# The first token half of a Winograd feed-forward: weight preparation placed at other steps, one subtraction on another engine, and an interleaved last period

## The chip, the cores and the metric

One core of a Trainium2 chip runs the whole block. The metric is the device time of one execution in microseconds. TensorE (PE) multiplies, VectorE (DVE), ScalarE (ACT) and GpSimd (POOL) do the element work, and SyncE (SP) issues almost all DMAs from one queue, in order.

## The reference

```python
mod = (_silu(c) @ w_mod).reshape(c.shape[0], 6, 1, -1)
sa, ca, ga, sb, cb, gb = (mod[:, j] for j in range(6))
h = _layernorm(x, axis=-1) * (1 + ca) + sa
x = x + ga * _A_ref(h, A_wq, A_wk, A_wv, A_wo, A_beta)     # segmented attention with a memory
h = _layernorm(x, axis=-1) * (1 + cb) + sb
x = x + gb * ((_silu(h @ B_w_gate) * (h @ B_w_up)) @ B_w_down)
```

There are 2048 tokens of width 576, and the feed-forward is 4608 wide. All data are float32. The attention fills about the first 650 us. The change lies in the feed-forward, which fills the rest, and in the last few microseconds ahead of it.

## The kernel before

**Two token halves, 18 periods each.** The feed-forward runs over token halves t = 0 and 1 (1024 tokens each). A period p takes 256 of the 4608 columns. In it, z = 0 is the gate and z = 1 the up projection. Each is computed as a 2 x 2 block product by the Strassen-Winograd scheme: seven products m = 1 to 7 in place of eight, each of a sum of activation blocks with a sum of weight blocks. So a period has 14 steps, k = 0 to 13, seven for z = 0 and then seven for z = 1. In the first half the order is `MO0 = (1, 2, 6, 7, 4, 5, 3)`, in the second `MO7 = (1, 5, 6, 2, 7, 4, 3)`.

**A product.** `prod` issues seven matmuls of 512 columns. A float32 operand is split into a rounded part and a remainder (`wh` and `wl` for weights; the activations `y` hold both), which gives three matmuls for each of two 128-row blocks, and one more for the last 32 rows, whose parts are packed in `wr`. In the first half the result goes to one of four PSUM banks `M` in rotation, and DVE (`sg`, `tb`, `tc`, `cu`, lines 1150 to 1191) or ACT (`tb`, line 1180, at m = 1) reads it. Combining the products gives the four blocks of the gate (`sg`, with a SiLU on ACT) and of the up projection; the gate times the up projection (L1159) is the input of the down projection, split into `ah` (ACT, L1226) and `al` (DVE, L1227) by `prep_a`.

**The down projection of a period runs in the next one.** In the first half `plain` issues it as 8 chunks of 12 matmuls of 288 columns, one chunk in each of steps 4 to 11; after each, DVE adds the result to `acc` (L1287). So steps 4 to 11 are long for PE and steps 0 to 3, 12 and 13 short. In the second half `down` uses the Winograd scheme (14 chunks of 6 matmuls), but for the last two periods.

**Weight preparation in the first half.** For each z, `load_o` fetches four raw weight blocks into `O` (two buffers); `sum_o` (four operations on POOL, L1091) makes the three sums. `prep_w` casts one operand to `wh` (ACT, L1100) and leaves the subtraction `wl` (DVE, L1101) in a list `later`, which is run at the start of the next step; it works `PF = 5` steps ahead with `WR = 8` buffers. `prep_r` casts the last rows into `wr` (ACT, L1085), and the subtraction of its 32 remainder rows runs on POOL (L1086). For the down weights, `load_d` fetches, `mul_d` scales them (POOL, L1114), `sum_d` makes sums for the second half (POOL, L1119), and `prep_d` casts `dh` (ACT) and subtracts `dl` (DVE, L1126) into a ring of 8. `store_o`, `store_r` and a store of `RW` write the sums to DRAM (`oD`, `rD`, `wdD`), where the second half reads them, so POOL has no work there.

**The second half's activations.** Also during the first half, the generator `prep2` normalizes the second token half, transposes it on PE (into a bank `M`), splits it and stores it in DRAM (`yD`). It is advanced by one piece at steps `G2` of periods 1 to 17, and its rest is run at the start of period 17. In period 17, once the z = 1 product m has used its operand, `load_y` overwrites that part of `y` with the second half's.

**What sets the order.** The order of the instructions on every engine is the order in which the program issues them, written out by hand, step by step. A tile ring makes a new tile wait for the readers of the one that it replaces. SP's queue holds each DMA until its operands are ready, and everything behind it waits too.

The steps of the first half, as the main loop has them (the work that a later listing moves is shown alone):

```python
if k == 7 - PF:
    load_o(tn, nx, 0)
elif k == 14 - PF:
    load_o(tn, nx, 1)
if tn == 0 and 4 <= k < 8:
    sum_o(nx, 0, k - 4)
elif tn == 0 and k >= 11:
    sum_o(nx, 1, k - 11)
elif k == 0 and p:
    sum_o(p, 1, 3)
```

Of the kernel before, what the change touches and what calls it, by code (L numbers as in the profile page):

```python
# [11 lines left out]
ALU = mybir.AluOpType  # L12
# [20 lines left out]
MO = [0, 76, 228, 380, 532]  # L33
WR = 8
PF = 5
NSG = 7
CH = (1, 1, 1, 1, 2, 1, 0, 1, 1, 1, 1, 2, 1, 0)
# [32 lines left out]
def f32(ap):  # L70
    return ap.bitcast(F32)
# [3 lines left out]
def block(ctx: ExitStack, tc: tile.TileContext, x, wqk, wv, wo, beta, wgu, wd, c, w_mod, out):  # L75
# [8 lines left out]
    def chain(*g):  # L84
        for a in g:
            yield from a
# [992 lines left out]
    def prep_r(t, p, z):  # L1079
        R[z] = r = wrp.tile([P, 7, P], F32R, tag="wr", name="wr")  # L1080
        if t == 1:
            nc.sync.dma_start(f32(r[0:96]), rD[p][z])
            return
        o = O[p, z]
        nc.scalar.copy(r[0:96], o[0:96, :, 2, :])  # L1085
        later.append(lambda: nc.gpsimd.tensor_tensor(r[32:64], o[32:64, :, 2, :], f32(r[32:64]), op=ALU.subtract))  # L1086

# [79 lines left out]

    def fin0(z, ij, bank, add):
        fin(z, ij, bank, add)
        if z:  # L1170
            prep_a(par[0], ij, AC[ij])

    par = [0]

    def step0(z, m):
        bank = ps.tile([P, L], F32, tag="M", name=f"M{m}", bufs=4)
        prod(z, m, bank, True, True)
        if m == 1:
            T[0] = tmp("tb")
            nc.scalar.copy(T[0], bank)  # L1180
        elif m == 2:
            fin0(z, (0, 0), bank, T[0])
        elif m == 6:
            nc.vector.tensor_tensor(T[0], bank, T[0], op=ALU.add)
        elif m == 7:
            T[1] = tmp("tc")
            nc.vector.tensor_tensor(T[1], bank, T[0], op=ALU.add)
        elif m == 4:
            fin0(z, (1, 0), bank, T[1])
        elif m == 5:  # L1190
            nc.vector.tensor_tensor(T[0], bank, T[0], op=ALU.add)
            fin0(z, (1, 1), bank, T[1])
        else:
            fin0(z, (0, 1), bank, T[0])

# [77 lines left out]
    def plain(t, p, c):  # L1273
# [25 lines left out]
    with tc.manual_schedule():  # L1299
# [49 lines left out]
        load_o(0, 0, 1)  # L1349
        gt, gw = chain(tr[1], tr[2]), iter(MO0[:PF])  # L1350
        for i in range(4):
# [34 lines left out]
        x2p = pool(p6, "x2p")  # L1386
        ps = pool(p6, "psm", 1, space=PSUM)
# [4 lines left out]
        seq = [(t, p, z, m) for t in range(2) for p in range(NPR) for z in range(2) for m in (MO7 if t else MO0)]  # L1392
        prev = None
        n = 0
        for p in range(NPR):
            nx = (p + 1) % NPR
            tn = 0 if nx else 1
            par[0] = p % 2
            if p == NPR - 1:
                run(g2)  # L1400
            for k in range(14):
                z, m = k // 7, MO0[k % 7]
# [8 lines left out]
                if k == 7 - PF:  # L1411
                    load_o(tn, nx, 0)
                elif k == 14 - PF:
                    load_o(tn, nx, 1)
                if tn == 0 and 4 <= k < 8:
                    sum_o(nx, 0, k - 4)
                elif tn == 0 and k >= 11:
                    sum_o(nx, 1, k - 11)
                elif k == 0 and p:
                    sum_o(p, 1, 3)  # L1420
                if k == 0 and p == 0:
                    store_o(p, 0)
                elif k == 9 and tn == 0:
                    store_o(nx, 0)
                elif k == 3:
                    store_r(p, 0)
                    store_o(p, 1)
                elif k == 6:
                    store_r(p, 1)
                if k == 2:  # L1430
                    prep_r(0, p, 1)
                elif k == 9:
                    prep_r(tn, nx, 0)
                if prev is not None and DS <= k < DS + 8:
                    plain(*prev, k - DS)
                if k == 1:
                    load_d(0, p)
                elif k in (5, 6):
                    mul_d(p, k - 5)
                elif 8 <= k < 12 and p < NPR - 2:  # L1440
                    sum_d(p, k - 8)
                elif k == 13:
                    nc.sync.dma_start(wdD[p][:, :NS[p]], RW[p][:, :NS[p]])
                if 8 <= k < 12:
                    prep_d(p, ((k - 8) // 2, k % 2), k - 8)
# [8 lines left out]
        ps = pool(p4, "ps4", 1, space=PSUM)  # L1454
        for p in range(NPR):
            last = p == NPR - 1
# [4 lines left out]
            for k in range(14):  # L1461
                z, m = k // 7, MO7[k % 7]
                todo, later[:] = later[:], []
                if n + PF < len(seq):
                    prep_w(*seq[n + PF][1:])
                n += 1
# [33 lines left out]
                if is_plain(1, p):  # L1500
                    if k in (4, 5, 6, 7):
                        prep_d(p, ((k - 4) // 2, k % 2), k - 4)
                elif k >= 7:
                    prep_d(p, POS[k - 7], WSLOT[POS[k - 7]])
                for ij, kk, j in (((0, 0), 11, 1), ((1, 1), 12, 4), ((1, 0), 13, 2)):
                    if k == kk:
                        prep_a(p % 2, ij if is_plain(1, p) else j, AC[ij])
            PA.clear()
            PA.update(AC)
# [59 lines left out]
```

## Time and profile before

| what | us |
|---|---|
| runs: median (lowest to highest) | 1984.6 (1984.16 to 1990.09) |
| the profiled execution | 1984.65 |
| its span | 1982.9 |
| PE busy in the span | 1893.7 |
| DVE busy | 1596.6 |
| ACT busy | 889.1 |
| POOL busy | 649.0 |
| `wl` on DVE, L1101, 504 of them | 298.8 |
| `wr` subtraction on POOL, L1086, 36 of them | 77.1 |
| sums of `O` on POOL, L1091, 144 of them | 161.9 |

The span is the time from the first to the last instruction of the core; the rest of an execution's time lies around it. A busy time says how long an engine had an instruction in it, also one that was held up, so a long busy time is not all work. A matmul's time overlaps that of its neighbours. To see what limits a stage, read it by itself: the first half of the feed-forward runs from 656 to 1334 us of the span, the second from there to the end.

In the page's view of the span in 40 equal slices (49.6 us each), PE and DVE in tenths are:

```
PE   7999999999998799999999999988999999999998
DVE  7574267877886899998998989984888888888886
```

DVE is at 8 to 9 tenths in the first half's slices (14 to 26), and PE dips in slices 27 and 28, where the halves meet.

### The profile page before, as it was taken

The numbers are of one execution on the slowest core, as the hardware profiler recorded it, in microseconds if no ns is written. First come the engines' busy times: TensorE is split into PE (matmuls) and PEld (weight loads), VectorE is DVE, ScalarE is ACT, GpSimd is POOL, SyncE is SP. The second block draws the span as 40 slices with busy tenths as digits, with TensorE's granted clock in tenths as the row PEclk, the third lists the DMA queues.
The fourth block names the chain that finished last, engine by engine and source line by source line (L and its number), as shares of the span: only waits on it lengthen the run. The fifth ranks groups of instructions, "written<-read, shape, count | busy, mean of one in ns | idle before, by whom it ended". The sixth has DMA issues, their size and how long they took to land.

```text
span 1982.9 us, 31199 instructions
## 1 busy us (share of the span) xinstructions
PE 1893.7 (96%) x10927; PEld 1564.1 (79%) x10927; DVE 1596.6 (81%) x3375; ACT 889.1 (45%) x1928; POOL 649.0 (33%) x808
## 2 busy tenths in 40 slices
PE   7999999999998799999999999988999999999998
PEld 4888856676766688888888877877888888888888
DVE  7574267877886899998998989984888888888886
ACT  2222267767666343344344343333444544454442
POOL 5212235554536556556556645520000000000000
PEclk9999999999999899999999999998999999999999
DMA  7777564445435554464555545477434334343441
GB/s 226 245 232 248 204 177 130 140 137 156 129 100 146 203 186 163 158 207 144 195 159 164 195 140 163 149 234 255 148 126 145 127 128 143 105 148 112 147 148 48
DMA packets 147052, 322.63 MB, mean 163 GB/s; under 512 B 26256, under 2 KB 61456, under 8 KB 145424
## 3 DMA queue, kind: packets, MB, share of 16 engines
q1 hardware_dynamic: 144640, 314.71, 49.3%
q10 hardware_dynamic: 2256, 5.93, 0.8%
q8 instruction: 86, 1.41, 0.3%
q14 instruction: 70, 0.57, 0.1%
HBM read 201.80 MB, written 118.75 MB: 162 GB/s over the span
## 4 chain that ended last, share of the span: by engine, by line
PE 71%; DVE 17%; DMA 5%; issue 3%; ACT 3%; POOL 1%; SPq 0%; ACTq 0%; DVEq 0%; POOLq 0%
PE A L1136 12%; PE pd L1266 9%; PE M L1136 8%; PE pd L1283 8%; PE C L1136 6%; PE s L589 4%; PE av L609 4%; PE pp L101 4%; PE s L187 4%; PE B L1136 3%; DVE wl L1101 3%; PE pv L101 2%; PE pw L707 2%; DVE dl L1126 2%; DVE sg L1159 2%
## 5 line engine op out<-in xcount | busy, mean ns | idle before, releaser
L1136 PE MATMUL M<-y,wh 128*128 128x512 f32 x1008 | 362.6, 400 | 32.6 <-DVE cu L1158 23.9
L1101 DVE TENSOR_TENSOR wl<-O,wh 128x256 fp32r<-128x256 f32 x504 | 298.8, 593 | 4.2 <-ACT wh L1100 0.5
L192 DVE CUSTOM_DVE_ANT_0 junk<-s,tri 128x256 bf16<-128x256 f32 (+3 forms) x512 | 228.7, 487 | 77.8 <-PE s L187 69.0
L1136 PEld LDWEIGHTS M<-y,wh 128*128 128x128 f32 x1008 | 191.3, 190 | 85.9 <-issue 31.7
L1226 ACT CAST ah<-sg 128x512 fp32r<-128x512 f32 x192 | 118.8, 619 | 308.6 <-DVE sg L1159 248.8
L592 ACT ACTIVATE Pt<-s 128x512 f32<-128x512 f32 (+1 forms) x352 | 186.9, 559 | 88.0 <-PE s L589 72.8
L1136 PE MATMUL A<-y,wh 128*128 128x512 f32 x576 | 202.7, 392 | 0.0
L1136 PE MATMUL M<-y,wl 128*128 128x512 f32 x504 | 199.6, 396 | 0.0
L1100 ACT CAST wh<-O 128x256 fp32r<-128x256 f32 x504 | 198.3, 401 | 0.0
L1283 PE MATMUL pd<-dh,al 128*128 128x288 f32 x640 | 188.7, 295 | 1.4 <-DVE al L1227 1.4
L1283 PE MATMUL pd<-dh,ah 128*128 128x288 f32 x640 | 189.5, 296 | 0.2 <-DVE acc L1287 0.2
L1283 PE MATMUL pd<-dl,ah 128*128 128x288 f32 x640 | 188.9, 295 | 0.0
L1091 POOL TENSOR_TENSOR O<-O 128x384 f32<-128x384 f32 x144 | 161.9, 1132 | 76.0 <-DMA oD<-O 18.5
L1271 DVE TENSOR_TENSOR acc<-acc,pd 128x576 f32<-128x576 f32 x216 | 159.0, 748 | 23.5 <-PE pd L1266 21.9
L1287 DVE TENSOR_TENSOR acc<-acc,pd 128x576 f32<-128x576 f32 x156 | 116.2, 745 | 57.6 <-PE pd L1283 57.1
L1227 DVE TENSOR_TENSOR al<-sg,ah 128x512 fp32r<-128x512 f32 x192 | 141.8, 738 | 24.3 <-ACT ah L1226 24.0
L589 PE MATMUL s<-qs,ks 110*128 110x512 f32 (+2 forms) x384 | 150.7, 409 | 5.6 <-DMA qs<-mD 3.7
L187 PE MATMUL s<-ks,qs 108*128 108x256 f32 (+3 forms) x512 | 141.6, 328 | 3.1 <-DMA ks<-kD 1.1
L1086 POOL TENSOR_TENSOR wr<-O,wr 32x896 fp32r<-32x896 f32 x36 | 77.1, 2142 | 202.4 <-ACT wr L1085 187.8
L1151 ACT ACTIVATE sg<-sg 128x512 f32<-128x512 f32 x109 | 69.0, 633 | 158.2 <-DVE sg L1150 158.0
L1266 PE MATMUL pd<-dh,ah 128*128 128x288 f32 x448 | 132.7, 296 | 0.0
L1266 PE MATMUL pd<-dh,al 128*128 128x288 f32 x448 | 132.1, 295 | 0.0
(363 smaller groups left out, 4696.6 us busy)
## 6 DMA issues: line engine op xcount, KB each, us to landing
O<-in_wgu_dram SPq DMA_DIRECT2D x36, 768.0 KB
oD<-O SPq DMA_DIRECT2D x36, 576.0 KB
O<-in_wgu_dram SPq DMA_DIRECT2D x36, 576.0 KB
O<-oD SPq DMA_DIRECT2D x36, 576.0 KB
ks<-kD SPq DMA_DIRECT2D x68, 216.0 KB
qs<-qD SPq DMA_DIRECT2D x68, 216.0 KB
rD<-wr SPq DMA_DIRECT2D x36, 336.0 KB
wr<-rD SPq DMA_DIRECT2D x36, 336.0 KB
```

The source lines that it names most:

```text
L187: nc.tensor.matmul(bank[:, n * (h - h0):n * (h - h0) + n], lhsT=qst[b][0:108, h, 128 * i:128 * i + 128], rhs=kst[b][0:108, h // 2, 0:n], s ...
L192: nc.vector.tensor_tensor_reduce(junk[:, :n], bank[:, n * (h - h0):n * (h - h0) + n], tri[:, L - n:], 1.0, -3e38, op0=ALU.add, op1=ALU.max ...
L589: nc.tensor.matmul(bank[:, n * (g - h):n * (g - h + w)].rearrange("p (a b) -> p a b", a=w), lhsT=kst[u % NB][0:110, g // 2, 128 * j:128 * ...
L592: nc.scalar.activation(pt[:, h:h + per, :n], bank[:, :n * per].rearrange("p (a b) -> p a b", a=per), AF.Exp, scale=SCALE)
L1091: nc.gpsimd.tensor_tensor(o[:, d], o[:, a], o[:, b], op=op)
L1100: nc.scalar.copy(wh, o)
L1101: later.append(lambda: nc.vector.tensor_tensor(wl, o, f32(wh), op=ALU.subtract))
L1136: nc.tensor.matmul(bank, lhsT=a, rhs=b, start=(first and n == 0), stop=(n == 6), skip_group_check=not first)
L1227: later.append(lambda: nc.vector.tensor_tensor(al, src, f32(ah), op=ALU.subtract))
L1266: nc.tensor.matmul(pd[:, i, :288], lhsT=a[:, tk], rhs=w, start=(k == 0), stop=(k == 2))
L1271: nc.vector.tensor_tensor(o, o, pd[:, :, :288], op=ALU.add)
L1283: nc.tensor.matmul(pd[:, i, :288], lhsT=a[:, tk], rhs=w, start=(k == 0), stop=(k == 5))
```

## The change

Nothing is computed differently, and each engine has as many instructions as before, but for one kind: the 36 subtractions of `wr` in the first half go from POOL to DVE.

- **Look-ahead.** In the first half the weights are cast six steps ahead (`PF0 = 6`) instead of five, in 9 buffers instead of 8. The ring of `dh` and `dl` shrinks from 8 to 7.
- **Steps of the first half.** `load_o` goes out at steps 1 and 8 (2 and 9 before); the sums for z = 1 come at steps 9 to 12 (11, 12, 13 and 0 before); the `d` weights are loaded at step 12 of the period before (step 1), scaled at steps 0 and 1 (5 and 6), summed at 2, 3, 7 and 8 (8 to 11), split at 4, 5, 6 and 10 (8 to 11), and stored at 9 (13). `prep_r` for z = 1 comes at 3 (2). `store_o` and `store_r` move by two or three steps, and `prep2` is advanced at steps 1 to 10 (4 to 13).
- **Last period of the first half.** Its 14 products alternate between z = 0 and z = 1 by operand (`ZML`), so that the part of `y` that an operand uses is free, and its reload starts, from step 2 on. Two more tiles (`tz`, `tw`) hold z = 1's intermediate sums beside those of z = 0. The loads of the second half's first `O` go out at steps 7 and 8 (2 and 9), and of its first `wr` at step 11 (9).
- **First period of the second half.** z = 0 takes the products in the order `MOB = (1, 6, 2, 5, 7, 4, 3)`.
- **Stores of the first half's result**, in the second half's first period, are issued three steps after the sum that they store. In the second half's last two periods `prep_d` moves from steps 4 to 7 to steps 4, 5, 6 and 10.
- Ahead of the first period, six weights are cast instead of five.

```diff
-WR = 8
+WR = 9
 PF = 5
+PF0 = 6
-WW = (19, 23, 25, 27, 30)
+WW = (19, 23, 25, 26, 27, 30)
-G2 = (4, 5, 6, 7, 8, 9, 10, 11, 12, 13)
+G2 = (1, 2, 3, 4, 5, 6, 7, 8, 9, 10)
...
+    MOB = (1, 6, 2, 5, 7, 4, 3)
+    ZM = [(z, m) for z in range(2) for m in MO0]
+    ZML = [(0, 1), (0, 2), (1, 1), (1, 2), (0, 6), (0, 7), (1, 6), (1, 7), (0, 4), (0, 5), (0, 3), (1, 5), (1, 4), (1, 3)]
+    ZM1 = [(z, m) for z in range(2) for m in MO7]
+    ZMB = [(0, m) for m in MOB] + [(1, m) for m in MO7]
+
+    def order(t, p):
+        if t == 0:
+            return ZML if p == NPR - 1 else ZM
+        return ZM1 if p else ZMB
...
-        later.append(lambda: nc.gpsimd.tensor_tensor(r[32:64], o[32:64, :, 2, :], f32(r[32:64]), op=ALU.subtract))
+        later.append(lambda: nc.vector.tensor_tensor(r[32:64], o[32:64, :, 2, :], f32(r[32:64]), op=ALU.subtract))
...
+            T[z, 0] = tx.tile([P, L], F32, tag="tz", name="tz", bufs=1) if end and z else tmp("tb")
+            nc.scalar.copy(T[z, 0], bank)
...
-        if p == NPR - 1 and (t or c == 1):
-            store(t, b, h, d, c if t else None)
+        if p == NPR - 1:
+            if t:
+                store(t, b, h, d, c)
+            elif c == 1:
+                return lambda: store(t, b, h, d)
...
-        dp = pool(p4, "dp", 8)
+        dp = pool(p4, "dp", 7)
...
+        def ahead(pf):
+            nonlocal nw
+            while nw < len(seq) and nw <= n + pf:
+                prep_w(*seq[nw][1:])
+                nw += 1
+
+        load_d(0, 0)
...
-                prep_w(*seq[n + PF][1:])
+                ahead(PF if end and k > 6 else PF0)
                 n += 1
                 for f in todo:
                     f()
-                step0(z, m)
-                if p == NPR - 1 and z:
-                    load_y(ACT_OP[m])
...
+                step0(p, z, m)
+                if end:
+                    if z:
+                        load_y(ACT_OP[m])
+                    if k == 0:
+                        prep_r(0, p, 1)
+                    elif k == 7:
+                        load_o(1, 0, 0)
+                    elif k == 8:
+                        load_o(1, 0, 1)
+                        prep_a(p % 2, (0, 0), AC[0, 0])
+                    elif k == 11:
+                        prep_r(1, 0, 0)
+                else:
+                    if k == 1:
+                        load_o(0, nx, 0)
+                    elif k == 8:
+                        load_o(0, nx, 1)
+                    if k == 3:
+                        prep_r(0, p, 1)
+                    elif k == 9:
+                        prep_r(0, nx, 0)
+                if k < 2:
+                    mul_d(p, k)
+                elif k in (2, 3, 8, 7) and p < NPR - 2:
+                    sum_d(p, (2, 3, 8, 7).index(k))
+                if not end and 4 <= k < 8:
                     sum_o(nx, 0, k - 4)
...
+                elif not end and 9 <= k < 13:
+                    sum_o(nx, 1, k - 9)
+                if k in (4, 5, 6, 10):
+                    j = (4, 5, 6, 10).index(k)
+                    prep_d(p, (j // 2, j % 2), j)
                 if k == 0 and p == 0:
                     store_o(p, 0)
...
+                elif k == 1:
+                    store_o(p, 1)
+                    store_r(p, 0)
+                elif k == 7:
+                    store_r(p, 1)
+                elif k == 9:
+                    nc.sync.dma_start(wdD[p][:, :NS[p]], RW[p][:, :NS[p]])
+                elif k == 11 and not end:
                     store_o(nx, 0)
+                elif k == 12 and not end:
+                    load_d(0, nx)
...
-                        plain(*prev, chunk)
+                        f = plain(*prev, chunk)
+                        if f:
+                            late[k + 3] = f
                         chunk += 1
+                    if k in late:
+                        late.pop(k)()
...
-                    if k in (4, 5, 6, 7):
-                        prep_d(p, ((k - 4) // 2, k % 2), k - 4)
+                    if k in (4, 5, 6, 10):
+                        j = (4, 5, 6, 10).index(k)
+                        prep_d(p, (j // 2, j % 2), j)
```

More of the change, by code (lines that the diff above doesn't have):

```diff
@@ L1166, in block, with step0 @@
     B = {}
[L1168 to L1175, printed above, removed]
+    def step0(p, z, m):
         bank = ps.tile([P, L], F32, tag="M", name=f"M{m}", bufs=4)
         prod(z, m, bank, True, True)
+        end = p == NPR - 1
         if m == 1:
[L1179 to L1194, printed above, removed]
+            T[z, 0] = tx.tile([P, L], F32, tag="tz", name="tz", bufs=1) if end and z else tmp("tb")
+            nc.scalar.copy(T[z, 0], bank)
+            return
+        u = T[z, 0]
+        if m == 7:
+            T[z, 1] = tx.tile([P, L], F32, tag="tw", name="tw", bufs=1) if end and z else tmp("tc")
+            nc.vector.tensor_tensor(T[z, 1], bank, u, op=ALU.add)
+            return
+        if m in (5, 6):
+            nc.vector.tensor_tensor(u, bank, u, op=ALU.add)
+        if m != 6:
+            ij = {2: (0, 0), 4: (1, 0), 5: (1, 1), 3: (0, 1)}[m]
+            fin(z, ij, bank, T[z, 1] if m in (4, 5) else u)
+            if z and not (end and m == 2):
+                prep_a(p % 2, ij, AC[ij])
     def step(z, m):
@@ L1391, in block @@
         new_acc(accp, (2, 3, 4, 5))
-        seq = [(t, p, z, m) for t in range(2) for p in range(NPR) for z in range(2) for m in (MO7 if t else MO0)]
+        seq = [(t, p, z, m) for t in range(2) for p in range(NPR) for z, m in order(t, p)]
         prev = None
-        n = 0
+        n, nw = 0, PF0
+        def ahead(pf):
[4 more added lines that the diff above has]
+        load_d(0, 0)
         for p in range(NPR):
             nx = (p + 1) % NPR
-            tn = 0 if nx else 1
-            par[0] = p % 2
-            if p == NPR - 1:
+            end = p == NPR - 1
+            if end:
                 run(g2)
             for k in range(14):
-                z, m = k // 7, MO0[k % 7]
+                z, m = order(0, p)[k]
                 todo, later[:] = later[:], []
-                prep_w(*seq[n + PF][1:])
+                ahead(PF if end and k > 6 else PF0)
                 n += 1
@@ new lines, in block @@
+                if end:
+                    if z:
[18 more added lines that the diff above has]
+                        prep_r(0, nx, 0)
@@ L1434, in block @@
                 if prev is not None and DS <= k < DS + 8:
                     plain(*prev, k - DS)
[L1436 to L1445, printed above, removed]
@@ L1454, in block @@
         ps = pool(p4, "ps4", 1, space=PSUM)
+        late = {}
         for p in range(NPR):
@@ L1461, in block @@
             for k in range(14):
-                z, m = k // 7, MO7[k % 7]
+                z, m = order(1, p)[k]
                 todo, later[:] = later[:], []
-                if n + PF < len(seq):
-                    prep_w(*seq[n + PF][1:])
+                ahead(PF)
                 n += 1
@@ L1507, in block @@
                         prep_a(p % 2, ij if is_plain(1, p) else j, AC[ij])
+            for f in late.values():
+                f()
+            late.clear()
             PA.clear()
```

22 lines of the change are left out of this document (2 added, 20 removed).

## The prediction

> **What bounds the kernel now.** I read the busy time by stretch first, then the waits, then the engines' instructions in order of time. Steps are numbered 0 to 13 in a period, periods 0 to 35 (18 per token half).
>
> ```profile
> core 0: us, PE busy (x) PEld busy (x) DVE busy (x) ACT busy (x) POOL busy (x), PEclk, DMA share, GB/s
> 1291.10:1334.20 43.10, 37.32 (x195) 32.09 (x195) 34.86 (x59) 14.48 (x34) 7.86 (x6) 0.96 0.70 230
> 1334.20:1383.60 49.40, 37.63 (x195) 32.51 (x194) 21.35 (x41) 15.08 (x36) 0.00 (x0) 0.86 0.78 256
> 1383.60:1417.50 33.90, 33.90 (x183) 29.64 (x183) 28.51 (x55) 16.34 (x39) 0.00 (x0) 1.00 0.53 177
> 988.50:1024.00 35.50, 35.50 (x196) 31.27 (x196) 34.27 (x51) 15.77 (x36) 22.95 (x19) 1.00 0.48 155
> 949.40:988.50 39.10, 36.98 (x203) 31.77 (x202) 35.31 (x56) 15.58 (x35) 19.66 (x16) 1.00 0.56 194
> ```
>
> Each row is one period: length, then busy time of PE, PEld, DVE, ACT, POOL. Period 9 (988.5) is full of matmuls: 35.4 us is the floor of a first-half period. Period 8 is 39.1. Between starts of successive periods (first product matmul to first product matmul) periods 1 to 16 take 608.7 us, mean 38.04, so 42.2 us above the floor. Period 0 has no down products (floor 14 x 1.61 = 22.6) and takes 26.0: 3.4 lost. Period 17 (1291.1) loses 7.7, and 18 (1334.2), whose down work is still the first half's, loses 14.0. Periods 19 to 34 take 34.05 with PE never idle: nothing is to be had there. In all 67 us can be won.
>
> ```profile
> PE M L1136 <- DVE cu L1158: 19.8, 20, 3.2
> ACT ah L1226 <- DVE sg L1159: 217.1, 56, 11.1
> POOL wr L1086 <- ACT wr L1085: 152.5, 24, 13.1
> PEld M L1136 <- ACT tb L1180: 10.2, 13, 1.0
> ACT st L992 <- DMA yD<-st: 30.0, 12, 5.7
> ```
>
> These are waits from 700 to 1300 us (total, times, longest). PE, the engine to fill, waits for DVE's `cu`, and for ACT's `tb`, which stands behind `ah` casts that wait for DVE. PE's gaps all but all lie in steps 1 to 4: four banks M rotate, and step 3 needs the bank of the last step 13. From the order of time I took how long after PE ended a product its reader began (mean of periods 2 to 16): 0.7 us at step 7, 2.6 at 11, 4.1 at 12, 5.3 at 13. PE stalls when step 13's lag passes three short steps less one read, 3 x 1.61 - 0.68 = 4.15 us.
>
> ```profile
> 863.97 1.23 DVE L1227 TENSOR_TENSOR al<-sg,ah 128x512 fp32r<-128x512 f32 x1
> 865.12 2.37 DVE L1126 TENSOR_TENSOR dl<-dr__10657,dh 128x288 fp32r<-128x288 f32 x1
> 867.41 0.68 DVE L1184 TENSOR_TENSOR tb<-M,tb 128x512 f32<-128x512 f32 x1
> ...
> 864.73 2.45 POOL L1086 TENSOR_TENSOR wr<-O,wr 32x896 fp32r<-32x896 f32 x1
> ```
>
> DVE's `dl`, 0.45 us when alone, takes 2.37 and ends with POOL's `wr`. Splitting all DVE rows of 656 to 1334 us in this way: operations with both inputs in SBUF last 144 us longer than their shortest, all of it over POOL operations (44.9 over `wr`, 53.6 over the sums of `O`, 39.4 over the `d` rows); those that read PSUM (`cu`, `acc`, `tc`) do not stretch (0.741 us without POOL, 0.744 beside it for `acc`). So DVE loses 60% of POOL's 74.7 us in `wr`, and about 35% of the rest.
>
> ```profile
> DMA y<-yD: 10.4, 1
> DMA wr<-rD: 3.1, 2
> L1056 SPq DMA_DIRECT2D y<-yD x7: 319/320/320, 1316.5 to 1335.9; - x7
> ```
>
> From the tile `y`, 1290 to 1390 us: period 18 stands 10.4 us for the operand that product 5 reloads, its second step, though the load is among the last issued.
>
> **The change part by part.**
>
> *wr's subtraction, POOL to DVE* (36). DVE's price has no row at this size. `wl` takes 0.404 us for 256 columns, `al` 0.675 for 512: 1.06 ns a column, so 896 give 0.404 + 640 x 1.06 ns = 1.08 us, about 1.0 of it before the next may start. Bounds: 0.82 (896 columns at the 0.92 ns a column between `al`, 0.675 at 512, and `acc`, 0.734 at 576, with no start) and 2.12 (POOL's own). At 1.0, DVE gets 36 us more and 45 less blocking, but each `wr` can itself meet a POOL operation; at 35% some 8 us come back. DVE's total stays about even; what counts is where the work lies.
>
> *The steps' order.* Without blocking, steps at their start-to-start price (`wl` 0.36, PSUM reads 0.63, `al` 0.63, `dl` 0.39, `acc` 0.70, `wr` 1.0) need of DVE, against PE's 3.22 us in steps 4 to 11 and 1.61 in the others:
> - steps 0 to 3: 4.0 before and after;
> - 4 to 7: 6.8 before, 9.0 after (three `dl`, one `wr`), of 12.9;
> - 8 to 11: 9.8 before, 10.1 after;
> - 12 and 13: 5.5 before, 5.1 after, of 3.2 (a `dl` leaves step 12).
>
> Blocking: in steps 8 to 13 POOL had four sums of `d`, a `wr` and three sums of `O` (3.6 + 2.1 + 3.2 us); after, two of `d` and four of `O` (1.8 + 4.3), the latter by step 12. At 35 and 60% that is 3.7 before, 2.1 after. In steps 4 to 7 it falls from 3.8 (sums 4.3, `mul_d` 3.0, `wr` 2.1) to about 1.8. So the lag at step 7 grows by 2.2 - 2.0, some 0.5 once idle moments are counted; the four steps behind add 0.7 less; the last two rise 1.75 instead of 2.7: step 13's lag is 5.3 + 0.5 - 0.7 - 0.95 = 4.15, right at the limit. With the scatter of the traced periods (2.7 to 8.5) a mean at the limit leaves about 1.0 us of stall where 2.6 stood: -1.6 x 16 = **-26**. Bounds: 0 left (-42); +32 (first rival). Period 0 and the stage ahead of it gain a `wl` and a `wr` on DVE and lose POOL's 2.42 us `wr`: -1 (-3 to +2).
>
> *Moved past queues at no cost.* The transfers of `d` go out at step 12 and are wanted by POOL at step 0, by `prep_d` at step 4, 3.2 + 6.4 us later; the issue waits for the store of step 9 and `dl` of step 11, and behind it in SP's queue stands only the next `O`. In the trace 10.3 us pass from issue (845.2) to use (855.5); late, it holds POOL, then the sums of `O`, which have until step 8. `prep2` at steps 1 to 10 puts ACT's wait for the `st` store (2.5 us on average, 5.7 at most) into short steps: behind it stand `wh` casts, six steps ahead now, but no `tb`. Its transposes, five of twelve at steps 1 to 4, take a bank each where banks are short: up to 1.6 us each, +4, inside the scatter above. Rings of 9 and 7 and the later stores: covered by PE's full steps, 0 (to +2 if a store holds SP).
>
> *The last period.* The reloads of `y` begin at step 2 instead of 7, and product 5 is wanted fourth in period 18 instead of second: issued in step 11, it has steps 12, 13 and three of period 18, 1.61 x 3 + 3.2 x 2 = 11 us, for 1.2 MB. From 1307 to 1351 the queues moved about 13.3 MB, 300 GB/s, so 4 us alone and 9 behind `O`. But `wr` for period 18 now goes out behind that reload: 1.2 + 0.34 MB behind what is left of `O` (2.8 MB from steps 7 and 8), landing some 9 us after issue, wanted after 5: 1 to 4 us of PE standing, I take 2.5, plus 1 of slow clock. 14.0 lost become 3.5: **-10.5** (-14 to 0). Here the matmul behind the 10.42 us gap took 0.76 us against 0.39 later.
> The Trainium skill ("TensorE: Matmul & The Clock Gate", What's actually happening) says that idle time throttles PE and some 3.4 us of work frees it: with a gap below that the 1 us would be 0.
>
> Period 17 starts with `prep2`'s rest, which had to wait for POOL's late sums of `O`; POOL is now done by step 12, and no sums block its tail: 7.7 lost become 2.2, **-5.5** (-7.7 to +1).
>
> **Sum.** -26 - 1 - 10.5 - 5.5 = -43 on 1984.65 us, this execution's time (span 1982.9, 1.75 around it), the median of the runs being 1984.6: **1942**. Its own range 1921 (-42, -3, -13, -6) to 1966 (-10, 0, -6, -3).
>
> **Rivals.**
> 1. *DVE becomes the bound (slower).* Place: periods 1 to 16. DVE is busy 35.1 us of 38.04 there. If the 45 us of blocking stay, because other POOL work now meets the DVE rows that `wr` met, DVE has 35.1 + 2.0, with the same 2.9 us of waiting 40.0 a period: +32, +2 in period 0, -16 at the turn: **2002**. It turns slower when less than about 21 us (36 + 2 - 17) of the blocking goes. For: `wl` once waited 5.38 us through five POOL operations. Against: POOL loses 75 us outright, PSUM readers never block.
> 2. *Nothing won inside the period.* `wr` trades POOL's hold for DVE's own work and its own waits, and the backlog moves from steps 12 and 13 to 4 to 7: only the turn is won, -16: **1968**. For: DVE's totals are even by the sum above. Against: the stall depends on steps 12 and 13, which get lighter. The Trainium skill ("Perfetto Trace Analysis", Optimizing Scalar/DVE Operations) says that moving operations between GpSimd and DVE might not help, as they share a read port; the stretched `dl` above agrees with the sharing.
> 3. *The wait at the turn only moves.* `O` and `wr`, issued later, stop PE in periods 17 and 18 as `y` did: -26 - 1 + 0: **1957**. For: 13 MB in 50 us fill the queues either way. Against: the early reloads take empty slots.
> 4. *The order is not what it says*, as interleaving stalls on `tz`: 1 us a step of period 17, 14 back: 1956; little speaks for it.
>
> **How the numbers follow.** Forecast 0.60, rival 1 0.15, rival 2 0.12, rival 3 0.10, rival 4 0.03. A measurement here tells 0.3%, 6 us, from no change. Faster 0.81 (forecast, 3, 4 and nearly all of 2), same 0.05 (between 2 and 1), slower 0.14. The range, 1922 to 1977, leaves out rival 1 and the best end.
>
> **What would show it.** Right: periods 1 to 16 at 36 to 37 us; `PE M` waiting for `cu` below 10 us in the same 600; `wl`'s mean under 0.70 us (0.784 now); `wr` on DVE at 1.1 to 1.5; PE's wait for `y` under 1 us, one for `wr` of 1 to 4. Wrong: DVE over 36 us in each period, periods at 38 or more, or PE standing over 8 us between periods 17 and 18.

## The result, and the profile after

| | before | after |
|---|---|---|
| median of the runs compared (lowest to highest), us | 1985.6 (1984.2 to 1990.1) | 2032.3 (2030.1 to 2036.4) |
| the profiled execution / its span | 1984.65 / 1982.9 | 2030.05 / 2028.3 |
| up to the first product | 656.4 | 654.9 |
| period 0 | 26.0 | 25.1 |
| periods 1 to 16 together (mean) | 608.7 (38.04) | 662.2 (41.39) |
| periods 17 and 18 | 92.5 | 86.2 |
| from period 19 on | 599.3 | 599.9 |

The change makes the kernel slower: ratio 1.0234, 95% interval 1.0209 to 1.0259. The span grows by 45.4 us. Periods 1 to 16 lose 53.5, the turn from one half to the other (periods 17 and 18) wins 6.3, all else 1.8.

First the busy time by stretch of the changed kernel, one period a row (4, 5, 17 and 18; columns as before the change).

```profile
core 0: us, PE busy (x) PEld busy (x) DVE busy (x) ACT busy (x) POOL busy (x), PEclk, DMA share, GB/s
808.00:844.90 36.90, 36.41 (x199) 31.41 (x198) 35.17 (x53) 15.38 (x35) 17.30 (x16) 1.00 0.52 164
844.90:889.80 44.90, 37.92 (x195) 32.68 (x194) 35.67 (x57) 14.35 (x33) 18.66 (x17) 0.92 0.48 157
1342.20:1385.10 42.90, 37.19 (x196) 32.22 (x195) 31.68 (x54) 12.70 (x30) 3.29 (x2) 0.92 0.77 264
1385.10:1428.40 43.30, 37.94 (x196) 32.65 (x195) 20.76 (x41) 15.24 (x36) 0.00 (x0) 0.92 0.78 240
```

Period 4 takes 36.9 us, as the prediction has it, and period 5 takes 44.9 with the same DVE busy time (35.2 and 35.7). So DVE's work is not what grew. Periods 1 to 16 scatter from 37.0 to 46.3 us: 46.0, 41.5, 40.5, 37.0, 44.9, 37.8, 40.5, 40.3, 44.4, 39.2, 37.6, 40.8, 39.7, 44.7, 46.3, 41.2.

The same view over periods 1 to 16 as a whole, before the change and after:

```profile
682.40:1291.10 608.70, 582.97 (x3152) 502.55 (x3153) 566.60 (x834) 234.90 (x532) 339.03 (x284) 1.00 0.52 169
680.00:1342.20 662.20, 601.31 (x3152) 517.84 (x3153) 565.61 (x871) 236.43 (x535) 278.97 (x253) 0.96 0.48 158
```

DVE's time is the same in sum, too. Of the 53.5 us, PE stands idle for 35.2 more (60.9 against 25.7) and takes 18.3 more for the same 3152 matmuls, at a mean granted clock of 0.96 instead of 1.00 (the column before the last two).

The waits of the changed kernel from 700 to 1350 us (engine, operation, what it waits for: total us, times, longest) show a new kind:

```profile
ACT st L1004 <- DMA yD<-st: 70.7, 16, 7.7
...
PE pd L1288 <- DVE acc L1292: 29.1, 9, 5.2
DVE st L1008 <- ACT st L1004: 24.6, 5, 6.9
...
PE M L1148 <- DVE cu L1170: 11.5, 10, 2.8
...
DVE st L1024 <- DMA ha<-xD: 11.1, 3, 3.9
DVE st L1011 <- ACT st L1004: 10.4, 3, 6.4
PE pt L1048 <- DMA xb<-xh: 9.7, 3, 5.8
```

The line for `acc` before the change, 700 to 1300 us:

```profile
PE pd L1283 <- DVE acc L1287: 0.2, 1, 0.2
```

Read the chain from its end. PE stands 29.1 us at the matmuls of the down projection, waiting for `acc`, where it stood 0.2 before. DVE stands 24.6 + 10.4 us at its subtraction in `st`, waiting for ACT's cast. ACT's cast waits for the store of the previous `st`: 70.7 us, longest 7.7 (30.0 and 5.7 in 600 us before). The wait that the change was to shorten, `PE M` for `cu`, did shrink, from 19.8 to 8.7 over the same 700 to 1300 us (11.5 in the longer stretch shown). Two more lines are new: DVE waits for `ha` and PE's transposes for `xb`, both loads of `prep2`.

One such chain, period 5, in order of time (start, duration, engine, line, operation; in brackets how long the engine stood and for what):

```profile
853.31 0.42 DVE L1113 TENSOR_TENSOR wl<-O,wh 128x256 fp32r<-128x256 f32 x1
853.76 0.33 SPq L1081 DMA_DIRECT2D O<-in_wgu_dram  x1
...
855.08 0.44 SPq L1106 DMA_DIRECT2D rD<-wr  x1
855.57 14.78 SPq L1009 DMA_DIRECT2D yD<-st  x3
862.84 0.40 ACT L1004 CAST st<-ha 128x256 fp32r<-128x256 f32 x1 [7.54 <-DMA yD<-st]
863.27 0.42 DVE L1008 TENSOR_TENSOR st<-ha,st 128x256 fp32r<-128x256 f32 x1 [6.74 <-ACT st L1004]
866.20 0.74 DVE L1292 TENSOR_TENSOR acc<-acc,pd 128x576 f32<-128x576 f32 x1
867.00 0.61 PE L1288 MATMUL pd<-dh,ah 128*128 128x288 f32 x1 [5.21 <-DVE acc L1292]
```

Step 1 begins at 846.5, but its load of `O` leaves SP's queue at 853.76, when DVE's `wl` of that step, the last reader of the buffer, ends at 853.73: DVE is 5 us behind PE there. The stores of `O` and `wr`, now also in step 1, stand behind that load, so all leave within 1.8 us (853.76 to 855.52), and `prep2`'s store of `st` comes behind them. The transfers of the same kernel from 853 to 863 us (number, KB each) give the sizes:

```profile
O<-in_wgu_dram SPq DMA_DIRECT2D x1, 768.0 KB
oD<-O SPq DMA_DIRECT2D x1, 576.0 KB
rD<-wr SPq DMA_DIRECT2D x1, 336.0 KB
yD<-st SPq DMA_DIRECT2D x1, 256.0 KB
oD<-O SPq DMA_DIRECT2D x1, 192.0 KB
```

1872 KB (1.92 MB) go ahead of 256 KB. Busy time by stretch (the last column is GB/s):

```profile
855.50:862.50 7.00, 6.29 (x38) 5.37 (x36) 1.03 (x3) 0.00 (x0) 2.96 (x3) 1.00 0.83 301
862.50:866.00 3.50, 0.00 (x0) 0.00 (x0) 2.31 (x4) 1.86 (x4) 0.86 (x2) 0.75 0.22 75
```

At 301 GB/s the 1.92 MB take 6.4 us, and the `st` store lands only behind them. In these 7 us ACT does nothing at all (0.00), DVE 1.03 us, and PE uses up what it has; then PE stands while DVE works off what was queued. The Trainium skill ("DMA: Bandwidth & Descriptors") says that a DMA's semaphore wait happens on the issuing sequencer before dispatch (Anatomy of one DMA — SWDGE (gpsimd) path) and that each DMA engine consumes its ring's descriptors in order (Queues, rings and completion order). This trace agrees: the load leaves 0.03 us after the `wl` that it waited for has ended, and ACT's cast, which waits for the small store, starts 7.3 us after that store was issued, when the 1.92 MB are through.

The burst holds `prep2`'s loads as well. In period 1 a burst of the same four transfers leaves at 693.88 to 695.67 us and the load of `ha` at 695.72, and DVE stands 3.5 us for it; periods 2 and 3 show the same. In period 15 the loads of `xb` go out right behind a burst (1264.24 and 1264.73), and PE stands 5.8 us.

### The profile page after: what moved, and what is told of

It is laid out like the page before. It is cut to its first block, busy times and chain, and to the rows that moved or that the text cites. A ratio compares the mean times of both kernels' runs of the same rounds, so it can differ in the third digit from the quotient of the medians.

```text
span 2028.3 us, 30981 instructions
## 1 busy us (share of the span) xinstructions
PE 1911.1 (94%) x10927; PEld 1581.1 (78%) x10927; DVE 1592.9 (79%) x3411; ACT 890.5 (44%) x1928; POOL 580.1 (29%) x772
## 4 chain that ended last, share of the span: by engine, by line
PE 69%; DVE 17%; DMA 8%; issue 2%; ACT 2%; SPq 1%; POOL 1%; ACTq 0%; DVEq 0%; POOLq 0%
PE A L1148 12%; PE pd L1271 9%; PE pd L1288 9%; PE M L1148 7%; PE C L1148 6%; PE pp L102 4%; PE s L590 4%; PE av L610 4%; PE s L188 4%; DVE wl L1113 3%; PE B L1148 3%; PE pw L708 2%; DMA yD<-st 2%; PE pv L102 2%; DVE sg L1171 2%
## 5 line engine op out<-in xcount | busy, mean ns | idle before, releaser
L1113 DVE TENSOR_TENSOR wl<-O,wh 128x256 fp32r<-128x256 f32 x504 | 262.5, 522 | 2.3 <-ACT wh L1112 1.4
L1148 PEld LDWEIGHTS M<-y,wh 128*128 128x128 f32 x1008 | 195.5, 194 | 74.0 <-issue 19.4
L1288 PE MATMUL pd<-dh,ah 128*128 128x288 f32 x640 | 194.1, 303 | 29.1 <-DVE acc L1292 29.1
L1288 PE MATMUL pd<-dh,al 128*128 128x288 f32 x640 | 193.2, 302 | 1.4 <-DVE al L1232 1.4
L1288 PE MATMUL pd<-dl,ah 128*128 128x288 f32 x640 | 193.1, 302 | 0.0
L1292 DVE TENSOR_TENSOR acc<-acc,pd 128x576 f32<-128x576 f32 x156 | 116.7, 748 | 54.7 <-PE pd L1288 53.5
L1288 PEld LDWEIGHTS pd<-dh,ah 128*128 128x128 f32 x640 | 124.6, 195 | 39.0 <-DVE acc L1292 33.0
L1271 PE MATMUL pd<-dh,ah 128*128 128x288 f32 x448 | 132.8, 296 | 0.0
L1271 PE MATMUL pd<-dh,al 128*128 128x288 f32 x448 | 132.6, 296 | 0.0
```

What stands on the lines that cost most here:

```text
L1113: later.append(lambda: nc.vector.tensor_tensor(wl, o, f32(wh), op=ALU.subtract))
L1148: nc.tensor.matmul(bank, lhsT=a, rhs=b, start=(first and n == 0), stop=(n == 6), skip_group_check=not first)
L1271: nc.tensor.matmul(pd[:, i, :288], lhsT=a[:, tk], rhs=w, start=(k == 0), stop=(k == 2))
L1288: nc.tensor.matmul(pd[:, i, :288], lhsT=a[:, tk], rhs=w, start=(k == 0), stop=(k == 5))
```

## The experiments

Each ratio is to the kernel before on the same chip (medians of before 1987 to 1989 us, and 1985.6 in the comparison above). So a difference between the times of two runs can be some 4 us off, and a difference between their ratios is surer. "Periods" is the mean of periods 1 to 16 in the profiled execution, "turn" the sum of 17 and 18: 38.04 and 92.5 before, 41.39 and 86.2 after. The expectations name theories by letters; the text after each says in words what fell.

**prep2's pieces back at steps 4 to 13**, all else as after:

```diff
-G2 = (1, 2, 3, 4, 5, 6, 7, 8, 9, 10)
+G2 = (4, 5, 6, 7, 8, 9, 10, 11, 12, 13)
```

> Theory A (prep2's pieces in short steps): a store of prep2's st tile now queues behind the 2 MB that go out at step 1; ACT stands for it, DVE's st subtraction stands for ACT, the acc additions behind it keep both pd banks full, and PE stops in steps 4 to 8. With the pieces back at steps 4 to 13 and all else as changed, periods 1 to 16 fall from 41.4 us to 36 to 37.5, about 60 to 80 us in all: 1955 to 1975 us, below before. Theory B (DVE is the bound, by wr on it): nothing changes, 2032. Theory C (the loads, scalings and stores moved to steps 12, 0 and 1 are at fault by themselves): less than half comes back, 2010 or more.

1980.2 us, ratio 0.9952 (0.9937 to 0.9968): 52 us back by this line alone (56 by the ratios), and a small gain on before. That is above the 1955 to 1975 us that were expected. Its waits from 700 to 1330 us:

```profile
ACT st L1004 <- DMA yD<-st: 24.6, 9, 4.8
...
PE M L1148 <- DVE wr L1098: 8.6, 1, 8.6
```

DVE's subtraction in `st` stands 2.2 us in all, PE under 1 us for `acc`, and no engine stands for `ha` or `xb`. The 8.6 us for `wr` fall in period 17 and are taken up with the turn below. What remains of the change's gain is small: periods 37.71, turn 89.2.

**wr's subtraction back on POOL**, all else as after (`nc.vector` to `nc.gpsimd` in `prep_r`):

> wr's subtraction back on POOL, all else as changed. Theory A: the wait for the st store stays; POOL's 75 us return and hold DVE some 40 us more against 36 us less work on it, so 2025 to 2045 us. Theory B: the loss goes, 1985 to 2000. Theory C: 2025 to 2045, as A.

2036.3 us, 1.0226 (1.0204 to 1.0248); ACT's waits for `st` 63.4 us. The loss stays, so it is not DVE's new work.

**The other way round: the move alone, in the kernel before** (`nc.gpsimd` to `nc.vector` in `prep_r`):

> The kernel before with wr's subtraction on DVE and nothing else changed. My sum: 36 us more work on DVE and 40 to 46 us less blocking, so no change, 1980 to 1990 us. Theory B (DVE the bound): 2005 or more. A gain beyond that, 1965 to 1978, would say that the blocking sat at the steps that matter (wr runs on POOL at steps 4, 9 and 10).

1986.1 us, 0.9997 (0.9984 to 1.0011): no difference. The Trainium skill ("Perfetto Trace Analysis", Optimizing Scalar/DVE Operations) says that offloading between GpSimd and DVE might not help, since they share a read port. This run agrees: the work came to DVE and blocking went (`wl` takes 0.603 us in the first half instead of 0.756), and the sum is nothing that the runs can tell from zero.

**Two buffers for st**, all else as after:

```diff
-            st = x2p.tile([P, 2, 256], F32R, tag="st", name="st")
+            st = x2p.tile([P, 2, 256], F32R, tag="st", name="st", bufs=2)
```

> Two st tiles instead of one, so that a cast need not wait for the store just before it; all else as changed. Theory A: ACT's wait for the store (71 us in 650) falls below 15, the gaps ahead of pd go, those of prep2's transposes for their loads (10 us) stay: 1975 to 1995 us. Theories B and C: 2025 to 2035.

2005.5 us, 1.0078 (1.0061 to 1.0095). ACT's waits for `st` fall to 7.6 us and 27 of the 52 us are gone: the wait for the store is a cause, and not all of it. A second buffer does nothing for `prep2`'s loads behind the burst: DVE still waits 11.3 us for `ha` in periods 1 to 3, and PE 5.84 us for `xb` in period 15 (5.80 in the changed kernel). That these come of the burst too, the later runs show: with the stores at step 0 and the load at step 2, DVE waits for `ha` no more, and PE for `xb` 0.4 us in all.

**The pieces alone, in the kernel before:**

```diff
-G2 = (4, 5, 6, 7, 8, 9, 10, 11, 12, 13)
+G2 = (1, 2, 3, 4, 5, 6, 7, 8, 9, 10)
```

> The kernel before, with prep2's pieces alone moved to steps 1 to 10. Theory A: the same wait appears, behind the load of step 2 and the stores of step 3 instead of step 1: 20 to 55 us slower than before, 2005 to 2040. Theory B: no change, 1985. Theory C: no change to 10 us slower.

1982.7 us, 0.9970 (0.9954 to 0.9987): a miss. The pieces' place costs nothing by itself; with something else that the change moved it costs 52 us. ACT waits 47.5 us for `st` here, 5.9 at the longest, and PE only 2.9 for `acc`.

**The stores of O and wr back at step 3**, all else as after:

```diff
-                elif k == 1:
+                elif k == 3:
+                    store_r(p, 0)
                     store_o(p, 1)
-                    store_r(p, 0)
```

> The changed kernel with the stores of O and wr, which it issues at step 1, at step 3 again, where the kernel before has them; prep2's pieces stay at steps 1 to 10. Theory A2 (the loss needs both: prep2's first store of a period must queue behind those 1.1 MB and the load of O): ACT's wait for the st store falls from 71 us to 30 to 50 and the gaps ahead of pd go: 1980 to 2000 us. Theory C2 (the other transfers and POOL's moved work make it, the stores do not matter): 2025 to 2035.

2003.5 us, 1.0075 (1.0051 to 1.0099): 29 us back.

**POOL's scaling and sums of d at steps 4 to 9**, with the pieces at 4 to 13:

```diff
-                if k < 2:
-                    mul_d(p, k)
-                elif k in (2, 3, 8, 7) and p < NPR - 2:
-                    sum_d(p, (2, 3, 8, 7).index(k))
+                if k in (4, 5):
+                    mul_d(p, k - 4)
+                elif k in (6, 7, 8, 9) and p < NPR - 2:
+                    sum_d(p, k - 6)
```

(`prep_d` then comes at steps 6, 7, 8 and 10, its store at 10.)

> The version of 1980 us (pieces back) with POOL's scaling and sums of d at steps 4 to 9 instead of 0 to 3, 7 and 8, and the split of d at 6, 7, 8 and 10. Theory D (what was won at steps 12 and 13 was given back at 0 to 3, where POOL's scaling holds DVE just as it must drain its backlog: 2.6 us blocked there against 0.3 before): blocking in steps 0 to 3 falls below 0.5, lag at step 1 from 5.7 to about 4.5, periods from 37.7 to 36.5 to 37: 1960 to 1970 us. Theory E (what is left is DVE's total, it only moves on): 1976 to 1985.

1964.5 us, 0.9882 (0.9861 to 0.9903): 15.7 us better than with the pieces alone put back (14 by the ratios), periods 36.74. The scaling, the sums and the splits of `d` moved together here and weren't tried one by one. Over all DVE rows of periods 2 to 15, duration less the shortest of the kind, DVE is held up about 2.5 us a period in steps 0 to 3 with the scaling there (0.4 before the change), and 0.9 with it at 4 to 9. The reader of step 1's product comes 5.7 and 3.6 us after the product.

**No interleaving:** the run with the pieces put back, with the last and first period in the old orders.

```diff
-        if t == 0:
-            return ZML if p == NPR - 1 else ZM
-        return ZM1 if p else ZMB
+        return ZM1 if t else ZM
```

> The version of 1980 us with the old order of products in the last period of the first half and the first of the second. If the interleaving is worth what was forecast, the standstill for y of 10 us is back and wr's of 3.5 and DVE wr's of 8.6 go or stay: 1988 to 1995 us. If it is worth nothing, 1980.

1986.5 us, 0.9990 (0.9975 to 1.0004), against 1980.2: the interleaving is worth 6 us in the runs, and 9 by the turn (98.2 against 89.2). It takes period 18 from 54.8 to 42.7 us and costs 3 in period 17 (43.4 to 46.5).

**The pieces at 1 to 10 again, with the scaling late** (the run of 1964.5 with the changed kernel's `G2`):

> The changed kernel with POOL's scaling, sums and split of d at the later steps, and prep2's pieces left at steps 1 to 10. Theory A3 (two separate losses: the st wait costs some 50 us whatever POOL does, POOL's scaling at 0 to 3 some 15): 2032 - 15 = 2010 to 2020 us. Theory G (the st wait only hurts because DVE's backlog is not drained by then, so that with the scaling out of steps 0 to 3 most of it is covered): 1970 to 1995.

2021.9 us, 1.0166 (1.0147 to 1.0185): the loss is there without the scaling in steps 0 to 3 (PE's matmuls wait 33.3 us for `acc`, ACT 60.4 for the `st` store). Scaling and pieces lose separately.

**Pieces and stores together, in the kernel before:** `G2` at 1 to 10, and `store_o(p, 1)` and `store_r(p, 0)` at step 1.

> The kernel before with prep2's pieces at steps 1 to 10 (alone: 1982.7 us) and the stores of O and wr at step 1 instead of 3. Theory A2 (pieces and stores in one step are enough): ACT's wait for the st store rises from 47 to 60 to 75 us in 600 and the time to 2000 to 2025. Theory G (it takes POOL's scaling at steps 0 to 3 as well): 1980 to 1992.

1981.4 us, 0.9964 (0.9952 to 0.9977): no loss, so this pair isn't enough. There the load of `O` is at step 2, so it comes behind the stores and the `st` store of step 1, and holds neither. This left the load as the suspect.

**The pieces ahead of the step's loads and stores**, all else as after (`next(g2)` moved up to just behind `step0`):

> The changed kernel with one thing moved inside a step: prep2's piece is issued first, ahead of the step's loads and stores, instead of last. Theory H (place in SP's queue: in step 1 the load of O waits for DVE's wl, the stores of O and wr stand behind it, all 1.9 MB go out at once, and the st store is last): the st store of step 1 leaves ahead of them, ACT's wait falls from 71 us to below 40 in 650, its longest from 7.7 to about 4, and the gaps ahead of pd go: 1982 to 2000 us. Theory I (the short steps themselves, any order): 2020 to 2035.

2023.8 us, 1.0173 (1.0156 to 1.0191): a miss in time. Period by period it did what was expected: in periods 5, 9 and 14, where the `st` store falls in step 1, ACT's wait fell from 7.5, 7.7 and 7.5 us to 1.7, 1.7 and 1.3. But in periods 7, 12 and 16 that store falls in step 2, behind the burst, and ACT still waits 6.9, 7.3 and 6.7. There the cast of `wr` stands next behind ACT's waiting cast, and DVE's subtraction in `wr` waits for it; in period 7:

```profile
936.81 1.08 DVE L1098 TENSOR_TENSOR wr<-O,wr 32x896 fp32r<-32x896 f32 x1 [7.02 <-ACT wr L1097]
```

PE then stands 5.8, 5.7 and 5.2 us in these three periods, so what periods 5, 9 and 14 won was lost again. Not the order within a step, but the burst itself had to go.

**The stores at step 0, ahead of the waiting load:**

```diff
-                if k == 0 and p == 0:
-                    store_o(p, 0)
-                elif k == 1:
+                if k == 0:
+                    if p == 0:
+                        store_o(p, 0)
                     store_o(p, 1)
                     store_r(p, 0)
```

> The changed kernel with the stores of O and wr at step 0, ahead of the load of O that waits for DVE, instead of behind it at step 1. Theory H: 1.1 of the 1.9 MB are gone by the time of the st store, which waits behind 0.8 MB alone: ACT's longest wait 4 to 5 us, 1990 to 2010 us, like the stores at step 3 (2003). Theory I: 2020 to 2035.

1996.7 us, 1.0035 (1.0017 to 1.0054): 36 us back, the longest wait of ACT for `st` 4.2 us. 1104 KB of stores now leave before the load blocks the queue.

The 16 us that were left, against the run with the pieces put back, three more runs were to place: the scaling late as well, the load at step 2 as well (`if k == 1:` to `if k == 2:` ahead of `load_o(0, nx, 0)`), and both.

> The stores of O and wr at step 0 (1996.7 us) with POOL's scaling and sums of d at steps 4 to 9 as well; the pieces of prep2 stay at steps 1 to 10. What is left of the loss with the stores at step 0 is 16 us (1996.7 against 1980.2 with the pieces at 4 to 13). Theory J (joint): the rest arises because DVE, held by POOL's scaling in steps 0 to 3 (0.5 + 1.1 + 0.7 + 0.2 us a period), reaches step 4 late with the shorter waits for the st store on top; without the scaling the late pieces cost nothing, so 1964 to 1973, as with the pieces at 4 to 13 (1964.5). Theory L (the load): the rest comes from the 768 KB load of O itself, still released ahead of the st store; then the scaling is worth its own 10 to 16 us and the rest stays: 1978 to 1988.

> The stores of O and wr at step 0 and the first load of O at step 2, as before the change, with the pieces at steps 1 to 10 and the scaling at 0 to 3. Theory L: the load now goes out behind the st store of step 1 and the rest of the loss is gone: 1979 to 1986. Theory J: the scaling still holds DVE, so 1991 to 2001.

> All three: stores at step 0, load at step 2, scaling at steps 4 to 9. Theories J and L both say 1962 to 1970: the pieces at steps 1 to 10 then cost nothing. If it stays above 1975 neither load nor scaling holds the rest, and the pieces cost something of their own in these steps (a PSUM bank, ACT's and DVE's place).

1979.4 us (0.9952, 0.9931 to 0.9973), 1984.3 (0.9990, 0.9973 to 1.0007) and 1965.7 (0.9883, 0.9856 to 0.9910). The scaling gives its 17 us and no more, so the rest stays; the load at step 2 takes 12 of the 16 away (9 by the ratios). With both changes the runs show no cost of the pieces at steps 1 to 10: 0.9883 against 0.9882 with the pieces at 4 to 13 and the scaling late, though the stores and the load stand at other steps there. So most of the rest was the 768 KB load itself. SP's queue in period 5 of the run with the load at step 2:

```profile
849.15 0.37 SPq L1009 DMA_DIRECT2D yD<-st  x1
849.63 0.40 SPq L1081 DMA_DIRECT2D O<-in_wgu_dram  x1
```

The small store now leaves first. The waits of that run from 700 to 1350 us:

```profile
ACT st L1004 <- DMA yD<-st: 36.7, 16, 4.7
...
PE pd L1288 <- DVE acc L1292: 2.4, 3, 1.4
```

ACT still waits 16 times, 36.7 us in all, and hardly any of it reaches PE; DVE's `st` rows wait 3.0 us for ACT's in this run and 35.0 in the changed kernel. DVE runs behind PE, and what is over when DVE comes to its `st` costs nothing: of ACT's waits here, those at steps 8 to 11, up to 4.7 us, reached DVE not at all, and two of 1.8 us at step 5 reached it as 1.0. Period 5 takes 37.95 us here, 44.89 after.

**The turn**, on top of the scaling at 4 to 9 and the pieces at 4 to 13: the two reasons found for PE's wait for `wr` in period 17 (`prep2`'s rest ahead of it, and the early z = 1 product) are taken away, and `wr` for period 18 is loaded a step earlier.

```diff
-    ZML = [(0, 1), (0, 2), (1, 1), (1, 2), (0, 6), (0, 7), (1, 6), (1, 7), (0, 4), (0, 5), (0, 3), (1, 5), (1, 4), (1, 3)]
+    ZML = [(0, 1), (0, 2), (0, 6), (0, 7), (1, 1), (1, 2), (1, 6), (1, 7), (0, 4), (0, 5), (0, 3), (1, 5), (1, 4), (1, 3)]
...
-            if end:
-                run(g2)
...
-                    elif k == 11:
+                    elif k == 10:
                         prep_r(1, 0, 0)
...
-                if k in G2 and p > 0:
+                if end and k == 2:
+                    run(g2)
+                elif k in G2 and p > 0:
```

> The version of 1964.5 us with three edits at the turn: in the interleaved last period the first z = 1 product comes at step 4 instead of 2, prep2's rest is run at step 2 of that period instead of ahead of it, and the second half's first wr is loaded at step 10 instead of 11. Theory F (the 8.6 us standstill at step 2 of period 17 is wr's subtraction wanted before DVE has drained its backlog and prep2's rest, and the 5.1 us at period 18 is wr's load behind the reload of 1.2 MB): period 17 falls from 46.8 to 37 to 39, period 18 from 44.1 to 38 to 41: 1948 to 1956 us. If the standstills only move to the reload of y, 1960 or more.

1958.1 us, 0.9844 (0.9830 to 0.9859): faster than both kernels, 6.5 us below the run that it builds on. The turn takes 82.1 us instead of 90.9 (period 17 39.3 instead of 46.8, period 18 42.8 instead of 44.0). The time is just above the 1948 to 1956 us that were expected, and which of the three edits did how much wasn't tried.

## Why the prediction was wrong, by its own steps

**The step that failed** is "Moved past queues at no cost", its sentence on `prep2`: "behind it stand `wh` casts, six steps ahead now, but no `tb`", with no price on that wait: the +4 us named there is for the transposes' banks, and a store that holds SP was given +2 at most. It looked behind ACT's waiting cast on ACT only. DVE's subtraction in the same `st` waits for that cast, in order, with the `acc` additions behind it, and PE's two `pd` banks wait for these. It also took the wait from the trace of before (2.5 us on average, 5.7 at most), though what stood ahead of the store in SP's queue was moved too: "the later stores: covered by PE's full steps". It also priced the transposes by the banks that they take, and not by their loads, which queue behind the burst. The runs put about 52 us here (2032.3 against 1980.2): 36 by the stores in the burst, 12 by the load's own 768 KB, and some 4 by which the run with the load at step 2 as well still lies above the one with the pieces put back (by the ratios 40, 9 and 7).

**The steps' order, -26.** The lag at steps 12 and 13 fell, as forecast: with the pieces put back from 4.1 to 2.4 and from 5.3 to 4.6 us (4.15 forecast). But "steps 0 to 3: 4.0 before and after" counted DVE's work only, and no blocking, though `mul_d` and two `sum_d` were moved there: about 2.1 us a period more, a term that the sum left out. So only 0.33 us a period was won with the pieces put back, instead of 1.6. With the scaling at steps 4 to 9 it is 1.3: 36.74 against the 36.4 that the forecast amounts to.

**wr on DVE.** 1.08 us was worked out for it; the line's row in the changed kernel gives the shortest, middle and longest:

```profile
L1098 DVE TENSOR_TENSOR wr<-O,wr x36: 1080/1081/1793, 648.6 to 1351.6; 32x896 fp32r<-32x896 f32 x36
```

"DVE's total stays about even": 1596.6 us busy before, 1592.9 after. From 700 to 1300 us `wl` went from 0.784 to 0.629 us on average, below the 0.70 named, and all operations with both inputs in SBUF last 98 us longer in the first half than their shortest, 144 before. These steps were right, and the move alone is worth nothing, as the forecast's sum for it had it.

**The turn, -16.** It gave 6.3. The wait for `y` is gone, as forecast, and the one for `wr` stands in its place at 4.7 us (1 to 4 forecast). Period 18 was to lose 3.5 us and loses 7.9. From the tile `y` in the changed kernel, 1290 to 1440 us, what its readers waited for:

```profile
DVE wr L1098: 11.8, 2
...
DMA wr<-rD: 4.7, 1
```

Period 17 was to lose 2.2 us and loses 7.5 (42.9 against 35.4). The step missed that z = 1's `wr`, wanted at the eighth product before, is wanted at the third when the sets alternate, while its cast and subtraction stand behind the rest of `prep2` at the period's start: PE stands 5.7 us (half of the 11.8; the other half is its weight load's same wait). The last run moved both, and the turn then won 10.4. What period 17 was to win by POOL's earlier sums can be had without them: in the kernel before with the pieces alone moved it takes 37.3 us (43.1 before). The 13.3 MB that the step counts from 1307 to 1351 us are 14.3 in the trace, which changes nothing.

**The rivals.** Rival 1 named the right sign for the wrong cause: DVE is busy 35.4 us a period before and after (the prediction's 35.1 comes out for periods 2 to 16), and taking its new work away changes nothing. Its test, DVE above 36 us in each period, fails: 3 of 16 are above. Rival 2's core, that the move of `wr` wins nothing by itself, is what the move alone shows. Rival 3 is half right: the wait at the turn moved, but 6 us of it were won. Rival 4 falls, since the interleaving is worth 6 us where it is tried. The range left out what happened because no case held a wait that grows with what is put ahead of it.

**With all three faults mended** the kernel stands at 1958.1 us, 16 above the forecast. By the profiled executions periods 1 to 16 won 20.1 of 26 us and the turn 10.4 of 16; the stages ahead took 3.7 us longer. This last can't be told from scatter: the first product comes between 654.7 and 665.5 us in kernels that hardly differ ahead of it.

One single wait of 5 us, at `acc` in period 14 of the run with all three edits at steps 0, 2 and 4 to 9, is of another kind:

```profile
1174.41 7.51 DVE L1113 TENSOR_TENSOR wl<-O,wh 128x256 fp32r<-128x256 f32 x1
```

This `wl`, 0.42 us when alone, lasts through eight POOL operations in a row, which POOL starts after it stood 11.0 us for `wr`. Still open are the 4 to 7 us by which the run with the load at step 2 lies above the one with the pieces put back, and the shares of the three edits at the turn; no run was made for them.

## What to carry to other kernels

When a step is moved, look at each in-order queue that it enters, and ask of every instruction that can wait there what stands behind it, and behind those that wait for it on other engines. A DMA that waits for a lagging engine gathers the ones behind it and lets them go as one burst: put ahead of it what is ready and what others wait for. Count the blocking that a moved operation brings to the place where it goes, as well as what it takes from where it was.

## What the runs showed that was not expected

- A wait on an engine off the path shrinks at each engine that it passes, by the backlog that it finds there. In the changed kernel ACT's waits of 7.5 to 7.7 us in periods 5, 9 and 14 reached DVE as 6.4 to 6.9 and PE as 5.1 to 5.2; those of 5.8 to 6.2 in periods 7, 10, 12 and 16 reached DVE as 2.9 to 3.8 and PE as 3.1 or less; those at steps 10 and 11, up to 4.5, reached neither.
- A gap costs more than its length: after PE's 5.2 us in period 5 the next matmul took 0.61 us and those behind it 0.44, where 0.29 to 0.30 is usual, for about 4 us (867.0 to 871.2); the granted clock is 0.92 over the period, 1.00 in the period without a gap.
